# Two attentions ahead of a feed-forward layer, on one core: groups of 1920 tokens in four lanes of 480, turned by VectorE, in place of units of 960 turned by TensorE

## The chip, the cores and the metric

The kernel runs on one core of one Trainium2 chip. A core has five engines with a queue each: TensorE (PE, with its weight load PEld), VectorE (DVE), ScalarE (ACT), GpSimd (POOL) and SyncE (SP, which here only issues DMAs). Each executes its queue in the order in which the program wrote it. The metric is the device time of one execution in microseconds. The kernel before has a median of 1677.85 us over three runs (1677.34 to 1679.97).

## The reference

Four batches of 12480 tokens with 128 channels; 32 inducing vectors; a feed-forward layer with 2048 inner channels.

```python
def mab(q, kv):                       # softmax attention, keys = values
    s = scale * (q @ kv.transpose(0, 2, 1))
    s = s - s.max(-1, keepdims=True)
    a = np.exp(s)
    a /= a.sum(-1, keepdims=True) + 1e-09
    return a @ kv
h = mab(I, x)                         # first attention: 32 queries over 12480 tokens
attn = mab(x, h)                      # second: every token over the 32 rows of h
y = np.maximum(attn @ w_in, 0.0)
out = y * y @ w_out
```

The weights come as 64-bit floats. The first attention of a batch has to be complete (its softmax runs over all tokens) before the second can begin for any token of that batch.

## The kernel before

**Folding.** The second attention's output is `a @ h`, a weighted sum of 32 rows. So the kernel never forms it: once a batch's h is known, `first_end` computes hw = h x w_in (32 x 2048, L635 to L644), and the feed-forward layer's first product is a x hw with the 32 attention weights of each token as inputs. For accuracy the weights stand as high and low parts, stacked four times 32 on 128 partitions (the tile st), and hw likewise. In the second product w_out and the activations are split into high and low parts too, and three of the four products are summed.

**Tiling.** Each batch is 13 units of 960 tokens (UNIT = NT x TS = 8 x 120). A unit has four lanes of 240 tokens for the attentions, and two blocks of 480 tokens for the feed-forward layer, 104 blocks in all.

**First attention of a unit** (class First). SP loads x as 120 partitions x 8 rows of 512 B (xn, L426). The channels have to be on the partitions for the scores: the first batch's x is turned by PE (L466) and copied by ACT; later batches load 32 x 32 blocks (xb, L444) which VectorE transposes (xt, L448, 128 x 960). Four matmuls give the scores of the four lanes on 4 x 32 partitions (L481). Each lane has a running maximum of its own: VectorE's max (L494) and neg (L500), ACT's exp with its sum (L507) and the factor `fade` by which earlier sums shrink (L510). PE turns e (ep, L515), ACT copies it (et, L274), 16 matmuls add e x x per lane (`mix`, L539), and VectorE adds it up (hacc L551, zs L561).

**End of a batch** (`first_end`). The four lanes are merged: their maxima gathered (L587 to L595), a factor per lane (wq, L599), the total (L607 to L614) and the joining matmul (L622). Then hw.

**Second attention of a unit** (class Second). Scores from hT (L677), evicted by ACT (ss, L274), turned by PE (s2t, L696), then VectorE's max (mx, L703), sub (d, L707), ACT's exp (L710), VectorE's total (z, L714), POOL's z + 1e-9 (L718), reciprocal (L721) and norm (L724) on 120 x 256; PE turns them back (ap, L755), ACT or VectorE writes the high part (L274) and VectorE the low part (L765) of sw, 128 x 240 each. SP spreads sw to st by 16 DMAs of 32 x 240 (L771). Only the very first unit goes another way: its high and low parts are made ahead of turning back (sk, L732 and L736), the matmul that turns them also stacks them (L741), and ACT copies the result to st, with no DMA.

**Feed-forward layer of a block** (`ffn_block`). 16 matmuls of 480 columns give h (L899). ACT does relu (L912, 960 wide) and square (L928, 1920 wide); VectorE makes hi (L933) and lo (L938), 1920 wide, four of each per block; 48 matmuls add up op (L977); VectorE turns it (ob, L993) and SP stores it with four DMAs (L999).

**What sets the order.** Nothing is issued where it is written. Each piece is a task of one `Plan`, with an engine or a choice of two, an assumed length, a due time, its needs and the buffers that it takes. `Plan.run` simulates the engines and, per engine, takes of the tasks that could start at about the same time the one due first. The resulting order is the order of the queues. The feed-forward blocks have due times from a base (T_MAIN) and a period; within a block HI_DUE, LO_DUE, SQ_DUE and others offset them.

Of the kernel before, what the change touches and what calls it, by code (L numbers as in the profile page):

```python
# [165 lines left out]
def induced_attention_then_squared_relu_ffn(  # L166
# [13 lines left out]
    NP = NF // 2  # L180
    NU = N // UNIT
    Q = P // M
    scale = 1.0 / math.sqrt(C)
    NQ = NF // 4
    GB, HB, LB = 3, 2, 2
    PERIOD, START, T_MAIN, NARROW, STEP = 30500.0, 2600.0, 44000.0, -9000.0, 3000.0
    W_DUE = [14e3, 20e3, 28e3, 34e3, 50e3, 52e3, 56e3, 60e3]

    XT, OT, ST = ("ACT|DVE", "ACT|DVE"), ("ACT|DVE", "ACT|DVE"), "ACT|DVE"
    XT_EARLY = "ACT"  # L190

    ORDER = "x0 x1 x2 i0 x3 x4 x5 i1 x6 x7 x8 i2 x9 x10 i3 x11 x12 o0 o1 o2 o3".split()
    SPARE = (6, 7, 8)
    FIRST_PAIRS, LAST_PAIRS = 2, 1
    OB, SS, SS_NS = "DVE", "ACT|DVE", (255, 317)

    FUSED = set()
    POOL_HI = set()
    POOL_LO = set()
    FUSED_DUE = 3000.0  # L200
    STICK = 0.0
    JOIN_IN, REST_OUT, JOIN_OUT = "DVE", "DVE", "DVE"
    HALVES = True
    PATIENCE = (0.0, 0.0, 40.0)

    PAIR, PAIR_DUE = False, 3000.0
    MB = 2
    G1_DUE, SQ_DUE, HI_DUE, LO_DUE, OP_DUE = -2000.0, 6000.0, 5000.0, 6000.0, 10500.0
    WIDE_LATER, NEXT_FIRST, STEP_0 = 7000.0, 2000.0, 600.0
    OT_DUE, OTP_DUE, OSB_DUE, XT_DUE, FILL = 4000.0, 4000.0, 10000.0, 1000.0, 0.0  # L210
    LATE_RELU, LATE_HI = 250.0, 50.0
    LATE_G1, LATE_OT = 250.0, 400.0


    const = ctx.enter_context(tc.tile_pool(name="const", bufs=1))
# [28 lines left out]
    identr = const.tile([P, P], F32R, name="identr")  # L244
    nc.vector.tensor_copy(identr, ident)
# [20 lines left out]

    add = plan.add
    ENG = {
        "ACT": nc.scalar.copy, "DVE": nc.vector.tensor_copy,
        "POOL": lambda dst, src: nc.gpsimd.tensor_scalar(dst, src, 1.0, 0.0, ALU.mult, ALU.add),  # L270
    }

    def copy(task, dst, src):
        ENG[task.by](dst, src)  # L274

# [68 lines left out]
    def open_early():  # L344
        pools["hi"] = ctx.enter_context(tc.tile_pool(name="hi", bufs=HB))
        pools["lo"] = ctx.enter_context(tc.tile_pool(name="lo", bufs=LB))
        pools["early_scope"] = ExitStack()
        pools["early"] = pools["early_scope"].enter_context(tc.tile_pool(name="early", bufs=6, side="right"))
# [12 lines left out]
    def load_weights(due):  # L361
# [3 lines left out]
        for k in range(n):  # L365
            sl = slice(k * WCH, (k + 1) * WCH)

            def load(t, sl=sl):
                nc.sync.dma_start(t, w_in[:, sl].bitcast(I32).rearrange("p (n two) -> p n two", two=2))

            def use(v, needs, due, kw, sl=sl):
                def join():
                    on(t).tensor_add(w_in_sb[:, sl], v["a"].bitcast(F32), v["b"])

                t = add(JOIN_IN, length(JOIN_IN), join, due, needs, port=True, **kw)
                return t

            ins.append(weights(f"i{k}", load, use, due[k]))
        for k in range(n):
# [6 lines left out]
            def use(v, needs, due, kw, k=k):  # L386
# [14 lines left out]
                tr = add(REST_OUT, length(REST_OUT), rest, due, [t], port=True, **kw)  # L401
                tj = add(JOIN_OUT, length(JOIN_OUT), join, due, [tr], port=True, **kw)
# [6 lines left out]

    class First:
        def __init__(self, b, u, due, early=False, begun=None):

            self.b, self.u, self.early, self.n, self.begun = b, u, early, f"{b}_{u}", begun
            self.s = s = state.setdefault(b, {"xt": {}, "chain": None, "bxt": {}})
            self.home = "early" if early and u not in SPARE else "xn"
            self.bx = Buffer(self.home)
            self.bt = s["bxt"][u] = Buffer("xt")
            lead = 2500 if early else 8000  # L420

            def load():
                self.xn = (pools["early"] if self.home == "early" else xn_pool).tile(
                    [TS, NT, C], F32, tag="xn", name=f"xn_{self.n}"
                )
                nc.sync.dma_start(self.xn, x_v[b, u])  # L426

            loaded = add("SP", 2050, load, ORDER.index(f"x{u}") * 10.0 - 1000.0 if b == 0 else due - lead - 20000, takes=[self.bx], late=0)
            self.turned = []
            if not early:  # L430
                self.turned.append(self.turn_blocks(due - lead))
                return
# [20 lines left out]

        def turn(self, k, due, loaded):
            bank_ = Buffer("o" if self.early else "m")
            v = {}

            def turn():
                if k == 0:
                    self.xt = self.s["xt"][self.u] = xt_pool.tile([C, UNIT], F32, tag="xt", name=f"xt_{self.n}")  # L460
                if self.early:
                    v["tp"] = ps_o.tile([P, 512], F32, tag="o", name=f"xtp_{self.n}_{k}")
                else:
                    v["tp"] = bank(f"xtp_{self.n}_{k}")
                for t in range(4):
                    nc.tensor.transpose(  # L466
                        v["tp"][:, t * TS:(t + 1) * TS], self.xn[:, 4 * k + t, :], ident[:TS, :TS]
                    )

            def turned():  # L470
                copy(e, self.xt[:, k * BLK:(k + 1) * BLK], v["tp"][:, :BLK])

            t = state["turn"] = add("PE", 421, turn, due, [loaded, state.get("turn"), self.begun] + self.turned, mode="t",
                    takes=[bank_] + ([self.bt] if k == 0 else []), reads=[self.bx] + ([self.bt] if k else []))
            e = add(XT_EARLY if self.early else XT[k], (440, 567), turned, due + (600 if self.early else XT_DUE), [t], reads=[bank_, self.bt])
            return e

        def score(self, where):

            for q in range(Q):  # L480
                nc.tensor.matmul(  # L481
                    where[q * M:(q + 1) * M, :], indT,
                    self.xt[:, q * 2 * TS:(q + 1) * 2 * TS], start=True, stop=True,
                )

        def weigh(self, scored, where, bank_, due, pair=None):

            s, u, n = self.s, self.u, self.n
            v = {}
            prev = s.get("first")  # L490

            def top():
                v["mx"] = tiny.tile([P, 1], F32, tag="mx", name=f"mx_{n}")
                nc.vector.tensor_reduce(v["mx"], where(), axis=AX.X, op=ALU.max)  # L494

            def shift():

                self.neg = tiny.tile([P, 1], F32, tag="neg", name=f"neg_{n}", bufs=4)
                if u:
                    nc.vector.scalar_tensor_tensor(self.neg, v["mx"], -scale, prev.neg, ALU.mult, ALU.min)  # L500
                else:
# [582 lines left out]
```

## Time and profile before

| | |
|---|---|
| median of three runs | 1677.85 us (1677.34 to 1679.97) |
| the profiled execution | 1679.11 us, span in the trace 1677.3 us |
| mean granted TensorE clock | 0.994 |
| moved by DMA | 101.21 MB, mean 60 GB/s |
| feed-forward on VectorE | hi 476.1 us, lo 893.8 us of 1608.4 busy |

The costliest lines of PE and ACT (line, engine, operation, tiles, count, then busy us and mean ns of one, then idle time just before):

```profile
L912 ACT ACTIVATE g<-h 128x960 f32<-128x960 f32 x832 | 786.2, 992 | 30.3 <-PE h L899 18.6
L899 PE MATMUL h<-st,hw 128*128 128x480 f32 x1664 | 515.1, 388 | 7.0 <-ACT g L912 6.2
L977 PE MATMUL op<-lo,wo_hi 128*128 128x480 f32 x1664 | 476.4, 383 | 2.8 <-DVE lo L938 2.8
```

A matmul's duration overlaps its neighbours', so the durations of a PE line do not add up to time. Idle time of an engine that is not the bottleneck costs nothing. In groups of lines the number before the comma is the sum of durations, and on VectorE the durations overlap a little too.

### The profile page before, as it was taken

What the parts mean: (1) busy time and instruction counts of PE and PEld (TensorE: products, weight loads), DVE (VectorE), ACT (ScalarE), POOL (GpSimd) and SP (SyncE); (2) the same over time, 40 slices, a digit from 0 to 9 for tenths busy, and PEclk for the clock granted to TensorE, in tenths of its full rate; (3) what the DMA queues carried; (4) which work ended last, traced back from release to release, by engine and by line L of the source; (5) the groups of instructions that cost most, each with busy time, mean ns of one, the idle gap of its engine ahead of it and who ended that gap; (6) DMA issues with size and microseconds to landing.
All of it is one profiled execution on the core that took longest, in us unless ns stands there. A gap on an engine that the chain in (4) does not pass through costs nothing.

```text
span 1677.3 us, 24531 instructions
## 1 busy us (share of the span) xinstructions
PE 1631.7 (97%) x8799; PEld 1340.5 (80%) x8799; DVE 1608.4 (96%) x1619; ACT 1564.8 (93%) x1657; POOL 77.6 (5%) x57
## 2 busy tenths in 40 slices
PE   6699999999999999999999999999999999999998
PEld 4378888888878888888877888888887888888886
DVE  4899999999999999999999999999999999999998
ACT  5599999999989999999998999999998999999996
POOL 0000000000000000000000000000000000000000
PEclk9899999999999999999999999999999999999999
DMA  9733333323243334334324334334111111212121
GB/s 201 136 61 64 72 57 70 68 56 72 52 65 63 70 61 68 62 67 73 61 48 70 63 68 72 61 69 66 34 33 35 30 32 35 38 31 42 26 44 21
DMA packets 451380, 101.21 MB, mean 60 GB/s; under 512 B 372636, under 2 KB 450748, under 8 KB 451260
## 3 DMA queue, kind: packets, MB, share of 16 engines
q1 hardware_dynamic: 451260, 99.66, 33.2%
q8 instruction: 70, 1.15, 0.3%
q14 instruction: 50, 0.41, 0.1%
HBM read 48.94 MB, written 25.56 MB: 44 GB/s over the span
## 4 chain that ended last, share of the span: by engine, by line
PE 76%; DVE 12%; issue 5%; ACT 3%; DMA 2%; SPq 2%; DVEq 0%; ACTq 0%
PE op L977 52%; PE h L899 18%; DVE lo L938 5%; DVE hi L933 4%; PE na L677 1%; ACT g L912 1%; SPq L426 1%; PE nb L539 1%; ACT g L928 1%; PE na L481 1%; DMA hi_i<-in_moe_w_in_dram 1%; DMA xn<-in_x_dram 1%; SPq L771 1%; DMA xb<-in_x_dram 1%; PE s2t L696 1%
## 5 line engine op out<-in xcount | busy, mean ns | idle before, releaser
L938 DVE TENSOR_TENSOR lo<-g,hi 128x1920 fp32r<-128x1920 f32 (+1 forms) x419 | 893.8, 2134 | 15.9 <-DVE hi L933 0.5
L912 ACT ACTIVATE g<-h 128x960 f32<-128x960 f32 x832 | 786.2, 992 | 30.3 <-PE h L899 18.6
L928 ACT ACTIVATE g<-g 128x1920 f32<-128x1920 f32 (+1 forms) x419 | 763.4, 1823 | 3.4
L899 PE MATMUL h<-st,hw 128*128 128x480 f32 x1664 | 515.1, 388 | 7.0 <-ACT g L912 6.2
L933 DVE CAST hi<-g 128x1920 fp32r<-128x1920 f32 (+1 forms) x419 | 476.1, 1137 | 6.7 <-ACT g L928 6.1
L977 PE MATMUL op<-lo,wo_hi 128*128 128x480 f32 x1664 | 476.4, 383 | 2.8 <-DVE lo L938 2.8
L977 PE MATMUL op<-hi,wo_lo 128*128 128x480 f32 x1664 | 454.1, 382 | 0.0
L977 PE MATMUL op<-hi,wo_hi 128*128 128x480 f32 x1664 | 451.4, 385 | 2.1 <-DVE hi L933 1.9
L899 PEld LDWEIGHTS h<-st,hw 128*128 128x128 f32 x1664 | 307.1, 188 | 77.6 <-issue 15.2
L977 PEld LDWEIGHTS op<-lo,wo_hi 128*128 128x128 f32 x1664 | 309.1, 188 | 59.5 <-DVE lo L938 10.9
L977 PEld LDWEIGHTS op<-hi,wo_lo 128*128 128x128 f32 x1664 | 311.3, 188 | 49.8
L977 PEld LDWEIGHTS op<-hi,wo_hi 128*128 128x128 f32 x1664 | 307.7, 188 | 53.5 <-DVE hi L933 6.0
L718 POOL TENSOR_SCALAR z<-z 120x8 f32<-120x8 f32 x51 | 76.9, 1508 | 1536.5 <-DVE z L714 1536.5
L993 DVE STREAM_TRANSPOSE ob<-op 128x480 f32<-128x480 f32 (+1 forms) x105 | 70.2, 669 | 3.8 <-PE op L977 3.7
L448 DVE STREAM_TRANSPOSE xt<-xb 128x960 f32<-128x960 f32 x39 | 45.6, 1170 | 1.5 <-DMA xb<-in_x_dram 1.5
L274 ACT COPY ss<-na 128x240 f32<-128x240 f32 x52 | 19.4, 374 | 25.0 <-PE na L481 13.9
L539 PE MATMUL nb<-xn,et 120*32 120x128 f32 x752 | 33.1, 280 | 0.0
L677 PE MATMUL na<-xt,hT 128*32 128x240 f32 x416 | 32.7, 387 | 0.4 <-DVE hT L274 0.4
L539 PEld LDWEIGHTS nb<-xn,et 120*32 120x32 f32 x752 | 25.0, 110 | 7.2 <-issue 0.2
L274 ACT COPY xt<-xtp 128x480 f32<-128x480 f32 x26 | 14.5, 557 | 14.9 <-PE xtp L466 14.9
L515 PE MATMUL ep<-ident,e 128*120 128x128 f32 x104 | 20.7, 281 | 6.3 <-ACT e L507 6.3
L274 ACT COPY et<-ep 120x256 f32<-120x256 f32 x52 | 19.6, 378 | 6.8 <-PE ep L515 6.6
(107 smaller groups left out, 542.8 us busy)
## 6 DMA issues: line engine op xcount, KB each, us to landing
xn<-in_x_dram SPq DMA_DIRECT2D x52, 480.0 KB, 5.3
out_dram<-ob SPq DMA_DIRECT2D x412, 60.0 KB, 2.0
st<-sw SPq DMA_DIRECT2D x816, 30.0 KB, 1.8
xb<-in_x_dram SPq DMA_DIRECT2D x156, 120.0 KB, 3.6
hi_i<-in_moe_w_in_dram SPq DMA_DIRECT2D x2, 512.0 KB, 10.6
lo_i<-in_moe_w_in_dram SPq DMA_DIRECT2D x2, 512.0 KB, 11.0
hi_o<-in_moe_w_out_dram SPq DMA_DIRECT2D x2, 512.0 KB, 10.1
lo_o<-in_moe_w_out_dram SPq DMA_DIRECT2D x2, 512.0 KB, 7.7
```

The source lines that it names most:

```text
L274: ENG[task.by](dst, src)
L448: nc.vector.transpose(self.xt, v["xb"].rearrange("p r c -> p (r c)"))
L539: nc.tensor.matmul(where[q * M:(q + 1) * M, :], self.et[:, k, q * M:(q + 1) * M], self.xn[:, 2 * q + k, :], start=(k == 0), stop=(k == 1),)
L677: nc.tensor.matmul(where[q * M:(q + 1) * M, :], self.s["hT"][:, :M], self.s["xt"][self.u][:, q * 2 * TS:(q + 1) * 2 * TS], start=True, sto ...
L718: E.tensor_scalar(v["z"], v["z"], 1e-9, 0.0, ALU.add, ALU.add)
L899: nc.tensor.matmul(c["hp"][:, l, :BLK], s["hw"][:, f * P:(f + 1) * P], s["st", u][:, 2 * k:2 * k + 2].rearrange("p q k t -> p (q k t)"), s ...
L912: nc.scalar.activation(g, h, AF.Relu)
L928: nc.scalar.activation(v["g"][:, h], v["g"][:, h], AF.Square)
L933: ENG[by](v["hi"][:, h], v["g"][:, h])
L938: engine.tensor_sub(v["lo"][:, h], v["g"][:, h], v["hi"][:, h])
L977: nc.tensor.matmul(w["op"][:, :BLK], wo[:, 4 * j + l, :], v[name][:, l, :], start=(j == x == 0 and l == 0), stop=(j == NQ - 1 and x == 5 a ...
L993: nc.vector.transpose(w["ob"][:, rows].rearrange("p r c -> p (r c)"), w["op"][:, rows.start * S:rows.stop * S])
```

## The change

- A batch is now 6 groups of 1920 tokens and one of 960. A group has up to four lanes of 480 tokens, and a lane is a block of the feed-forward layer. x comes as 15 whole rows per partition (7680 contiguous bytes, L399).
- First attention (L495 to L564): one step for 1920 tokens. The running maximum is one for all lanes: after VectorE's max (top, L502) the lanes' maxima are spread by `lanes` (L506), gathered by a small matmul with `same` (L509), reduced (most, L513) and shifted (L520). e is turned by VectorE (L540) instead of by PE and ACT. 15 matmuls mix (L548).
- End of a batch (L587 to L624): since all lanes share a maximum, the merging of lanes falls away.
- Second attention (L657 to L705): scores of 128 x 480, turned by VectorE straight from PSUM (L664), max, sub, exp, total, norm on 128 x 480, turned back by VectorE (L692), high and low parts 480 wide, and four DMAs of 32 x 480 per lane. Each lane has a tile st of its own. The last group of a batch, 960 tokens, takes four lanes of 256 of which two overlap.
- The very first block has a short chain of its own (`mini`, four lanes of 128). It is spread by 16 DMAs which ACT's queue issues.
- The first batch's x is still turned by PE (15 turns per group, L437); its evictions may go to ACT or VectorE.
- The planner's numbers are set anew: HI_DUE from 5000 to 3000, LO_DUE from 6000 to 6500, OP_DUE from 10500 to 10300, PATIENCE, the loads' order and due times; xt has 14 half buffers, st six, `early` three, xn two, and a, sw one.

The diff, cut to its core:

```diff
-TS = 120
-NT = 8
-UNIT = TS * NT
-BLK = UNIT // 2
 S = 32
-NR = BLK // S
+NR = 15
+LANE = S * NR
...
-    G1_DUE, SQ_DUE, HI_DUE, LO_DUE, OP_DUE = -2000.0, 6000.0, 5000.0, 6000.0, 10500.0
+    G1_DUE, SQ_DUE, HI_DUE, LO_DUE, OP_DUE = -1500.0, 6000.0, 3000.0, 6500.0, 10300.0
+    PATIENCE = (20000.0, 60000.0, 40.0)
...
+                nc.sync.dma_start(
+                    self.xn[:R], x[b, self.at:self.at + self.L * LANE, :].rearrange("(p r) c -> p r c", r=NR)
+                )
...
+            def lanes():
+                v["lanes"] = tiny.tile([P, Q], F32, tag="lanes", name=f"lanes_{n}")
+                nc.vector.tensor_scalar_mul(v["lanes"][:R], lane_q[:R], v["mx"][:R])
+            def gather():
+                nc.tensor.matmul(v["sp"][:, LANE:LANE + L], same[:R, :], v["lanes"][:R, :L], start=True, stop=True)
+            def most():
+                v["top"] = tiny.tile([P, 1], F32, tag="top", name=f"top_{n}")
+                nc.vector.tensor_reduce(v["top"], v["sp"][:, LANE:LANE + L], axis=AX.X, op=ALU.max)
...
+            def turn_e():
+                self.et = att.tile([P, NR, S], F32, tag="et", name=f"et_{n}")
+                nc.vector.transpose(
+                    self.et[:R].rearrange("p r m -> p (r m)"), v["e"][:R].rearrange("p r t -> p (r t)")
+                )
...
+            def turn():
+                v["d"] = att.tile([P, NR, M], F32, tag="d", name=f"d_{n}")[:RW, :NB, :]
+                nc.vector.transpose(v["d"].rearrange("p r m -> p (r m)"), v["na"][:RW, :W])
...
+            def back():
+                v["a"] = att.tile([P, LANE], F32, tag="a", name=f"a_{n}", bufs=1)[:RW, :W]
+                nc.vector.transpose(v["a"], v["d"].rearrange("p r m -> p (r m)"))
...
+            def spread(k):
+                st = self.st[k] = st_pool.tile([P, LANE], F32R, tag="st", name=f"st_{b}_{g}_{k}")
+                for a in range(4):
+                    for i, c0, c1, d0 in to[k]:
+                        queue(
+                            st[a * M:(a + 1) * M, d0:d0 + c1 - c0].bitcast(F32),
+                            v["sw"][i * M:(i + 1) * M, a % 2, c0:c1].bitcast(F32),
+                        )
+            urgent = tag == "m"
+            queue = nc.scalar.dma_start if urgent else nc.sync.dma_start
```

What it does to the order. VectorE's queue in the middle of a batch, before (hi and lo are the feed-forward splits, ob the output's turn; the first three numbers are unit, block and quarter of the block's 16 inner tiles):

```order
L933 CAST hi_1_0_3_1403<-g_1_0_3_1358 128x1920
L938 TENSOR_TENSOR lo_1_0_3_1420<-g_1_0_3_1358,hi_1_0_3_1403 128x1920
L933 CAST hi_1_1_0_1438<-g_1_1_0_1375 128x1920
L938 TENSOR_TENSOR lo_1_1_0_1448<-g_1_1_0_1375,hi_1_1_0_1438 128x1920
L933 CAST hi_1_1_1_1467<-g_1_1_1_1412 128x1920
L993 STREAM_TRANSPOSE ob_1_0_1481<-op_1_0_1321 128x480
L938 TENSOR_TENSOR lo_1_1_1_1487<-g_1_1_1_1412,hi_1_1_1_1467 128x1920
```

The same queue after, also in the first batch (group in place of unit; lanes, top: first attention of the next batch; mx, d: second attention of this one):

```order
L785 CAST hi_2_2_3_2374<-g_2_2_3_2328 128x1920
L506 TENSOR_SCALAR lanes_3_2384<-lane_q,mx_3_2354 128x4
L668 TENSOR_REDUCE mx_0_4_2386<-d_4_2292 128x15
L790 TENSOR_TENSOR lo_2_2_3_2392<-g_2_2_3_2328,hi_2_2_3_2374 128x1920
L785 CAST hi_2_3_0_2406<-g_2_3_0_2362 128x1920
L513 TENSOR_REDUCE top_3_2415<-sp_3_2311 128x1
L671 TENSOR_TENSOR d_4_2292<-d_4_2292,mx_0_4_2386 128x480
L790 TENSOR_TENSOR lo_2_3_0_2421<-g_2_3_0_2362,hi_2_3_0_2406 128x1920
```

In the first piece a hi is twice followed at once by its own lo; in the second short attention steps stand between the two.

ACT's queue ahead of the first relu of the feed-forward layer, before (hw and wo_hi: folding and weight splits; st: the first unit's attention weights, written by ACT):

```order
L507 ACTIVATE e_1_0_889,z_1_0_888<-na_1_0_871,neg_1_0_885 128x240
L274 COPY et_0_901<-ep_0_896 120x256
L274 CAST st_0_922<-ap_0_0_911 128x4x120
L274 CAST st_0_922<-ap_0_1_916 128x4x120
L391 CAST wo_hi<-lo_o_732 128x512
L274 COPY ss_1_952<-na_1_929 128x240
L912 ACTIVATE g_0_0_0_957<-h_0_0_0_927 128x960
```

and after:

```order
L619 CAST hw_711<-wp_3_749 128x512
L361 CAST wo_hi<-lo_o_595 128x512
L705 DMA st_0_0_782<-sw_0m 32x128 x3
L705 DMA st_0_0_782<-sw_0m 32x96
L705 DMA st_0_0_782<-sw_0m 32x128 x3
L705 DMA st_0_0_782<-sw_0m 32x96
L705 DMA st_0_0_782<-sw_0m 32x128 x3
L705 DMA st_0_0_782<-sw_0m 32x96
L705 DMA st_0_0_782<-sw_0m 32x128 x3
L705 DMA st_0_0_782<-sw_0m 32x96
L767 ACTIVATE g_0_0_0_809<-h_0_0_0_800 128x960
```

Two copies by ACT have become 16 DMA issues on ACT's queue, ahead of the first relu.

SP's queue where the first batch goes over into the second, before (st: attention weights of the second batch's first unit; xb: blocks of x for the third batch, x4 and x16 are counts of DMAs):

```order
L999 DMA out_dram<-ob_11_1_4685 32x15x32 x4
L444 DMA xb_2_4767<-in_x_dram 32x30x32 x4
L771 DMA st_0_4819<-sw_0_4795 32x240 x16
L999 DMA out_dram<-ob_12_0_4881 32x15x32 x4
L426 DMA xn_3_4935<-in_x_dram 120x8x128
```

and after:

```order
L844 DMA out_dram<-ob_5_3_4272 480x1x32 x4
L469 DMA xb_1_0_4340<-in_x_dram 32x15x32 x8
L705 DMA st_0_0_4385<-sw_0_4361 32x480 x4
L705 DMA st_0_1_4393<-sw_0_4361 32x480 x4
L705 DMA st_0_2_4404<-sw_0_4361 32x480 x4
L705 DMA st_0_3_4415<-sw_0_4361 32x480 x4
L844 DMA out_dram<-ob_6_0_4494 480x1x32 x4
```

The 16 DMAs ahead of the next batch's first h have become four for each of its four blocks; eight loads of xb stand ahead of them where four stood.

More of the change, by code (lines that the diff above doesn't have):

```diff
@@ L478, in score @@
[L478 to L490, printed above, removed]
+            t = state["turn"] = add("DVE", 1090, turn, due, [t, state.get("turn"), self.begun],
+                                    takes=[self.bt[h]], reads=[bb])
@@ new lines, in weigh @@
+            t = add("DVE", wide_ns(LANE), top, due + step, [t, back("shifted")], reads=[bank_])
+            t = add("DVE", 100, lanes, due + step, [t])
+            t = add("PE", 70, gather, due + step, [t], reads=[bank_])
+            t = add("DVE", 100, most, due + step, [t], reads=[bank_])
+            t = self.shifted = add("DVE", 70, shift, due + step, [t])
+            cl = add("POOL", 100, clear, due, [back("totalled")]) if R < P else None
+            t = self.powered = add("ACT", 820, power, due + 2 * step, [t, cl, back("powered")], takes=[be], reads=[bank_])
@@ L661, in first_end @@
             bw = Buffer("m" if b else "h")
[L662 to L664 removed]
+            d = due + 2 * step + k * step
+            t = add("PE", 870, lambda k=k: wide(k), d, [s["joined"], w_ins[k]], takes=[bw])
+            t = add("ACT", 520, lambda k=k: part(k), d, [t], reads=[bw])
@@ L795, in weigh @@
-            t = add("DVE", 340, top, d + max(step, PAIR_DUE if pair else 0), [t], reads=[bt])
-            td = add("DVE", 340, sub, d + max(step, PAIR_DUE if pair else 0), [t], reads=[bt])
-            tp = add("ACT", 307, power, d + 2 * step, [td])
-            t = add("DVE", 330, total, d + 2.5 * step, [tp])
-            ez = add("DVE" if first else "POOL", 150, safe, d + 2.5 * step, [t])
-            t = add("DVE", 120, invert, d + 2.5 * step, [ez])
-            tp = add("DVE", 340, norm, d + 3 * step, [t], port=True)
@@ L816, in weigh @@
-            t = add("PE", 219, back, d + 4 * step, [tp], takes=[ba], mode="t")
-            th = add(ST, (255, 317), high, d + 5 * step, [t], takes=[bw], reads=[ba])
-            tl = add("DVE", 317, low, d + 5 * step, [th], reads=[ba, bw])
-            t = None
-            for q in range(Q):
-                t = add("SP", 2200, lambda q=q: spread(q), d + 6 * step, [tl, t], late=0,
-                        takes=[] if q else [self.bst], reads=[bw] + ([self.bst] if q else []))
-            self.ready = [t] * 2
@@ new lines, in __init__ @@
+            t = add("DVE", ns, turn, d + step, [t], takes=[bd], reads=[bank_])
+            t = add("DVE", ns, top, d + 1.5 * step, [t], reads=[bd])
+            t = add("DVE", ns, sub, d + 2 * step, [t], reads=[bd])
+            t = add("ACT", wide_ns(W, "ACT"), power, d + 3 * step, [t], reads=[bd])
+            t = add("DVE", ns, total, d + 4 * step, [t], reads=[bd])
+            ez = t = add("DVE" if urgent else "POOL", 150, safe, d + 4 * step, [t])
+            t = add("DVE", 100, invert, d + 4 * step, [t])
```

679 lines of the change are left out of this document (274 added, 405 removed).

## The prediction

> **What bounds the kernel now.** I read first the page's totals and slices, then the windows by stage, then VectorE's timeline.
>
> ```profile
> PE 1631.7 (97%) x8799; PEld 1340.5 (80%) x8799; DVE 1608.4 (96%) x1619; ACT 1564.8 (93%) x1657; POOL 77.6 (5%) x57
> DVE  4899999999999999999999999999999999999998
> ```
>
> Three engines are above 93%, so totals do not name the bound; the slices only say that the start is the one loose place. The windows (window, length, busy and count of PE, PEld, DVE, ACT, POOL, granted clock, DMA share, GB/s) split it:
>
> ```profile
> 0.00:11.00 11.00, 4.29 (x22) 2.79 (x23) 1.33 (x8) 2.96 (x4) 0.70 (x6) 1.00 0.86 158
> 11.00:47.00 36.00, 27.50 (x338) 19.42 (x341) 21.77 (x65) 23.33 (x68) 0.00 (x0) 1.00 1.12 225
> 47.00:74.70 27.70, 16.10 (x131) 8.71 (x123) 24.67 (x61) 12.30 (x31) 0.00 (x0) 0.83 0.74 132
> 74.70:102.00 27.30, 24.23 (x122) 17.62 (x123) 22.05 (x27) 23.96 (x30) 1.08 (x1) 0.92 0.25 43
> 102.00:455.00 353.00, 351.75 (x1928) 290.53 (x1927) 349.58 (x351) 338.97 (x349) 16.96 (x11) 1.00 0.36 66
> 455.00:525.00 70.00, 67.22 (x347) 53.40 (x346) 66.23 (x70) 61.69 (x69) 3.42 (x3) 0.98 0.38 64
> 832.00:894.00 62.00, 59.73 (x317) 46.80 (x315) 58.13 (x64) 53.60 (x58) 0.24 (x1) 1.00 0.34 59
> 1204.00:1330.00 126.00, 124.53 (x622) 101.48 (x621) 121.22 (x115) 118.52 (x118) 5.50 (x4) 1.00 0.17 32
> 1330.00:1671.00 341.00, 339.91 (x1617) 283.86 (x1615) 331.49 (x276) 327.47 (x306) 14.86 (x10) 1.00 0.18 34
> ```
>
> In the main phase (102 to 455) PE and VectorE both have 99%. Which of them waits, the timeline tells (start, duration, engine, line):
>
> ```profile
> 249.54 2.16 DVE L938 TENSOR_TENSOR lo<-g,hi 128x1920 fp32r<-128x1920 f32 x1
> 251.62 1.15 DVE L933 CAST hi<-g 128x1920 fp32r<-128x1920 f32 x1
> 252.88 2.16 DVE L938 TENSOR_TENSOR lo<-g,hi 128x1920 fp32r<-128x1920 f32 x1
> 254.95 1.15 DVE L933 CAST hi<-g 128x1920 fp32r<-128x1920 f32 x1
> 256.02 0.67 DVE L993 STREAM_TRANSPOSE ob<-op 128x480 f32<-128x480 f32 x1
> 256.62 2.12 DVE L938 TENSOR_TENSOR lo<-g,hi 128x1920 fp32r<-128x1920 f32 x1
> ```
>
> Each instruction starts about 0.08 us before the one ahead ends: lo 252.88 to 254.95 is 2.07, duration 2.16; the transpose 0.60 for 0.67. So an instruction costs its duration less 0.08; I call that its slot. The one exception is a hi followed at once by its own lo: 251.62 to 252.88 is 1.26, against 1.07 for the next hi, which has a transpose behind it. In the main phase VectorE's instructions add up by slots to the elapsed time, 61.2 us for every four blocks, so **VectorE's queue is the bound** there, and PE is fed just in time. Outside it VectorE is short of work at the start (11 - 1.33 = 9.7, then 14.2, 3.0 and 5.3: 32.2 us), at three batch turns (3.8, 3.9 and 4.8 us) and in the last batch (9.5 of 341).
>
> **The change, by VectorE's slots.** Rows that price it (busy, mean ns | idle before):
>
> ```profile
> L938 DVE TENSOR_TENSOR lo<-g,hi 128x1920 fp32r<-128x1920 f32 x413 | 887.0, 2148 | 15.8 <-DVE hi L933 0.5 <-PE op L977 0.5
> L938 DVE TENSOR_TENSOR lo<-g,hi 128x960 fp32r<-128x960 f32 x6 | 6.8, 1152 | 0.0
> L993 DVE STREAM_TRANSPOSE ob<-op 128x480 f32<-128x480 f32 x103 | 69.5, 674 | 3.0 <-PE op L977 2.9
> L703 DVE TENSOR_REDUCE mx<-s2t 120x8 f32<-120x256 f32 x52 | 21.7, 417 | 3.1 <-PE s2t L696 2.8
> L714 DVE TENSOR_REDUCE z<-d 120x8 f32<-120x256 f32 x52 | 21.1, 406 | 0.5 <-ACT d L710 0.5
> L765 DVE TENSOR_TENSOR sw<-ap,sw 128x240 fp32r<-128x240 f32 x51 | 20.3, 399 | 0.7 <-ACT sw L274 0.7
> L494 DVE TENSOR_REDUCE mx<-na 128x1 f32<-128x240 f32 x39 | 15.4, 394 | 0.3 <-ACT ss L274 0.3
> L551 DVE SCALAR_TENSOR_TENSOR hacc<-hacc,fade,nb 128x128 f32<-128x128 f32 x43 | 14.5, 337 | 0.3
> L561 DVE SCALAR_TENSOR_TENSOR zs<-zs,fade,z 128x1 f32<-128x1 f32 x44 | 9.3, 211 | 3.2 <-ACT fade L510 3.1
> L721 DVE RECIPROCAL z<-z 120x8 f32<-120x8 f32 x52 | 9.2, 176 | 0.5 <-POOL z L718 0.4
> L500 DVE SCALAR_TENSOR_TENSOR neg<-mx,neg 128x1 f32<-128x1 f32 x48 | 7.2, 151 | 0.0
> L274 DVE CAST sw<-ap 128x240 fp32r<-128x240 f32 x14 | 5.6, 401 | 0.1
> L587 DVE TENSOR_SCALAR lanes<-lane_q,neg 128x4 f32<-128x4 f32 x4 | 0.9, 219 | 0.0
> L595 DVE TENSOR_REDUCE negt<-lp 128x1 f32<-128x4 f32 x4 | 0.6, 158 | 0.5 <-PE lp L591 0.4
> ```
>
> *Removed.* First attention, 52 units: maximum 52 x 0.315 = 16.4, hacc 13.1, zs 6.6, neg 52 x 0.07 = 3.6, together 39.7. Second attention: max, sub and norm 52 x 3 x 0.337 = 52.6, total 52 x 0.326 = 17.0, reciprocal 5.0, low 51 x 0.319 = 16.3, high 14 x 0.32 = 4.5, the first unit's sk about 1.0: 96.4. The merging of lanes at a batch's end about 1.3. Sum **137.4**.
>
> *Added.* Between the two lo rows an element costs (2148 - 1152) / 960 = 1.04 ns, so a 480-wide maximum is 394 + 250 - 80 = 0.564 us, sub, norm, total and low 0.56 to 0.57; a 480 transpose is the output's, 0.594. First, 28 groups: maximum 0.564, lanes 0.139, most 0.078, neg 0.07, turned e 0.594, hacc 0.257, zs 0.131: 1.83 each, 51.3. (A last group of a batch has half the lanes but the same width, so its maximum and turn save nothing.) Second, 24 full groups: two transposes, max, sub, total, norm, low, reciprocal: 4.11 each, 98.7; four half groups of 256 width 2.51 each, 10.0; the small first chain 1.7; high on VectorE 1.8. Eleven and eight evictions of the first batch's turned x, 5.8. Sum **169.3**, so +31.9. None of the 480-wide transposes from SBUF stands in the trace; bounds are the 0.33 us slot of a 256-wide row and a second 0.594: 80 of them at -0.26 to +0.6 would be -21 to +48. The output's row has their very width, so I take it, and allow +-8.
>
> *Won by order.* By the program's order 165 of the 413 wide hi stood directly ahead of their own lo; now 61 do, since short attention steps lie between. 104 x 0.19 = **-19.8**. So VectorE's own work rises by 12.1, and nearly all of that lies ahead of the fifth block; the main phase stays as it is.
>
> The Trainium skill, "VectorE: DVE Perf Modes", section "Rules for kernel authors", says the contrary of this step: a drain follows every VectorE instruction however instructions are chained, so that only their number matters. The 1.26 against 1.07 above disagrees; by the page the sum would be 19.8 higher.
>
> *PE and ACT* lose work: the turns of e and scores through PE with their evictions. That is off VectorE's queue and I cost it at nothing; cover is VectorE itself.
>
> *Start.* Loads of x come in 512 B rows before and in 7680 B pieces after. Two windows, x alone and w_out:
>
> ```profile
> 38.00:42.00 4.00, 2.93 (x38) 1.81 (x38) 1.93 (x6) 2.58 (x8) 0.00 (x0) 1.00 1.16 186
> 44.00:50.00 6.00, 3.72 (x51) 2.45 (x51) 4.39 (x13) 4.61 (x15) 0.00 (x0) 1.00 1.08 311
> ```
>
> The first batch is 6.4 MB: 34 us at 186 GB/s, 21 at the other rate. Of the 14.2 us idle in 11 to 47 I let 8 go. Against that the first block was handed from PSUM by ACT alone; now it crosses by 16 DMAs on ACT's queue. Their price is SyncE's (issue min/median/max ns, landing us):
>
> ```profile
> L771 SPq DMA_DIRECT2D st<-sw x816: 507/588/1849, 90.1 to 1629.6; - x164
> DMA to landing us min/median/max: 1.7/1.8/3.8
> 467.57 11.76 SPq L771 DMA_DIRECT2D st<-sw  x16
> ACT ss L274 <- PE na L481: 4.3, 1, 4.3
> ```
>
> 16 x 0.588 = 9.4, landing 1.8, relu and exp queued on ACT behind the issues 2.4, less 3.4 of loose work for VectorE, so the third window's idle goes from 3.0 to about 11, the fourth from 5.3 to 4, the first stays: 9.7 + 6.2 + 11 + 4 = 30.9, **-1**.
>
> *Turns.* At 467.57 the second batch's first spread issues 16 DMAs in 11.8 us (row three), and ACT waits 4.3 us at once (row four). Now the four DMAs of lane 0 suffice, 2.4 us, so the next h may start some 9 us sooner; the eight loads of xb stand ahead of them on SyncE, 4.7 us, and by the order the attention's last VectorE step has 3 to 4 us less VectorE work between itself and the next batch's first hi (13.5 us for 17.5 at the first turn). The three windows lack 12.5 us of busy VectorE, plus the lost overlaps of 0.08, say 14; I leave 1 us per turn: **-11**. In the last batch, 9.5 idle in 341 is 2.8% against 1.0% in the main phase, an excess of 6; half of it goes, **-3**.
>
> Sum: +12.1 - 1 - 11 - 3 = -2.9 on the profiled execution's 1679.1 (span 1677.3 and 1.8 around it): 1676.2. That execution is 1.25 above the median of the runs, 1677.85, so **1675.0**.
>
> **Rivals.**
> *Loads no quicker.* The 8 us at the start stay: 1683. It needs x to come at 186 GB/s whatever the row. The 311 of the next window, where rows are longer, speaks against it; that these are other tensors, for it. The Trainium skill, "DMA: Bandwidth & Descriptors", section "Specifications", puts the least size for line rate at 512 B, by which the old rows lost nothing. The rate of 186 disagrees.
> *Slower: the handoff on ACT's queue.* All of the first h waits for 16 issues, and ACT issues nothing else meanwhile. At 1.2 us each it is 19.2 instead of 9.4: 1685; at the row's largest, 1.849, 20 more: 1695. It decides from (6.2 + 9.4) / 16 = 0.98 us each, where the time passes 1681.2. For it: no DMA issued by ACT is in the trace, and w_out's splits are still on ACT. Against: the median.
> *Order wins nothing.* If hi's 0.19 is paid by whatever comes next, 19.8 are lost: 1695. The row of the 1.07 speaks against it. (It is the first page's rule.)
> *PE is the bound after all.* Then its lost turns shorten the main phase:
>
> ```profile
> L515 PE MATMUL ep<-ident,e 128*120 128x128 f32 x104 | 20.7, 281 | 6.3 <-ACT e L507 6.3
> L696 PE MATMUL s2t<-ident,ss 128*120 128x128 f32 x104 | 20.1, 275 | 0.0
> L755 PE MATMUL ap<-ident,d 120*128 120x120 f32 x102 | 18.9, 266 | 0.0
> ```
>
> 59.7 us of overlapping durations, some 40 net, less what more VectorE work takes back: about -23, 1652. The fit by slots speaks against it.
> *A quick handoff.* At 0.35 us an issue and less idle elsewhere in the start, -11: 1664.
>
> **How the numbers follow.** Chances: forecast 0.57 (own range 1667 to 1683, mostly from the transposes' +-8), loads 0.12, handoff 0.11, order 0.08, PE 0.07, quick handoff 0.05. For 0.8 I leave out PE's case and the upper ends beyond 1692: 1659 to 1692. What a measurement here can tell from no change is 0.2%, that is 1674.5 to 1681.2. Of the forecast's 0.57 I put 0.29 below, 0.20 within, 0.08 above; loads 0.04 within and 0.08 above; handoff 0.02 and 0.09; order 0.01 and 0.07; PE and quick handoff 0.12 below, less 0.01 within. Faster 0.40, same 0.28, slower 0.32.
>
> **What would show it.** Slots of 0.59 for the new transposes, and of 0.56 to 0.57 for the other 480-wide steps; a hi with a step between it and its lo at 1.07; x at near 300 GB/s from 11 us on; 16 ACT-issued DMAs in about 9.4 us ahead of the first h; the first output's turn near 102 as before; turns at which VectorE lacks about 1 us. I am wrong if the main phase, with VectorE full all the same, moves away from 61 us per four blocks, or if the first h stands far from the 74.7 us at which the third window ends.

## The result, and the profile after

| | before | after |
|---|---|---|
| median | 1678.38 us (1677.34 to 1679.97, 4 runs) | 1688.18 us (1685.36 to 1689.74, 4 runs) |
| profiled execution | 1679.11, span 1677.3 | 1689.74, span 1687.9 |
| mean granted clock | 0.994 | 0.982 |

The ratio is 1.0056 (95% interval 1.0038 to 1.0073): the change is slower by about 10 us, where 1675.0 was forecast. The time lies inside the stated range, on the wrong side of no change. One execution of a later run (two buffers sw) took 2633.84 us at a granted clock of 0.557, for 1680.63 to 1684.8 of its other nine; its ratio leaves that one out.

The page's totals after, then the same windows as before:

```profile
PE 1629.7 (97%) x8146; PEld 1299.7 (77%) x8146; DVE 1623.4 (96%) x1524; ACT 1533.8 (91%) x1443; POOL 72.0 (4%) x38
DVE  7699999999999999999999899999999999999998
```

```profile
11.00:47.00 36.00, 30.39 (x336) 18.59 (x328) 31.81 (x92) 18.66 (x53) 0.10 (x1) 0.96 0.71 217
47.00:74.70 27.70, 12.83 (x74) 4.84 (x74) 21.81 (x49) 6.31 (x13) 0.00 (x0) 0.62 0.24 79
74.70:102.00 27.30, 16.10 (x44) 11.59 (x45) 15.35 (x19) 15.64 (x18) 1.44 (x2) 0.63 0.31 58
102.00:455.00 353.00, 352.68 (x1808) 286.86 (x1807) 351.30 (x316) 338.44 (x313) 13.93 (x6) 1.00 0.33 68
1330.00:1671.00 341.00, 337.58 (x1524) 279.28 (x1517) 331.64 (x255) 329.35 (x290) 15.80 (x5) 0.99 0.17 33
```

VectorE is full again in the main phase, and fuller in the second window (31.8 us busy for 21.8). Over the third and fourth together it lacks more (17.8 us for 8.3). PE's granted clock is 0.62 and 0.63 there, with PE busy 12.8 and 16.1 us; before it was 0.83 and 0.92, with 16.1 and 24.2. What that clock costs was not taken apart.

Windows cut the stages at the old boundaries, so a second reading is wanted: how much work VectorE's queue holds up to a given output, and how long it took. I give every VectorE instruction its slot (start to start, by form; 0.19 us more where it reads what the one just ahead wrote), add them up in queue order to each block's output turn, and set that beside the turn's end in the trace. What is left is idle time of VectorE (us). The split turns on the slots taken: with the median start to start of each form in its own trace, VectorE's work rises by 2.5 in place of the 7.6 below and its idle time by 8.6 in place of 3.5, so single entries hold to some 5 us.

| up to | before: work | idle | after: work | idle |
|---|---|---|---|---|
| first block's output | 69.6 | 33.0 | 83.5 | 32.0 |
| 24th, just ahead of the first turn | 423.8 | 31.8 | 434.4 | 31.8 |
| 32nd, behind the first turn | 549.6 | 36.1 | 558.8 | 36.9 |
| 56th, behind the second | 922.4 | 39.7 | 928.5 | 41.4 |
| 84th, behind the third | 1340.9 | 43.2 | 1356.1 | 42.4 |
| last | 1625.7 | 45.6 | 1633.3 | 49.1 |

Work rose by 7.6 and idle by 3.5: 11.1, which is the difference of the last output's turn (1682.4 against 1671.3). Up to the first turn the sums are as forecast: more work and the start's idle about the same. But the turns still cost 10.6 (11.4 before) where 1 each had been expected, and the last batch 6.7 for 2.4. With the other slots the turns cost 11.5 (9.5 before) and the last batch 7.2 for 2.3, so by either count the forecast gain is missing.

What waits there, by VectorE's own waits in the trace of after (us in total, times, longest):

```profile
DVE z L678 <- ACT d L674: 11.3, 1, 11.3
DVE xt L241 <- ACT xt L241: 6.8, 5, 4.7
DVE hi L785 <- ACT g L780: 5.4, 7, 1.5
DVE sw L241 <- DMA st<-sw: 4.5, 2, 3.8
DVE xt L472 <- DMA st<-sw: 4.5, 2, 3.2
DVE xt L472 <- DMA xb<-in_x_dram: 2.7, 1, 2.7
```

The first row is the handoff at the start. The last three are new or larger (before, only 1.5 us for xb): VectorE, the bound engine, waits for DMAs that SyncE issues. Behind the first turn, VectorE and then SyncE (SPq: DMA issues) in the trace of after:

```profile
531.19 1.15 DVE L785 CAST hi<-g 128x1920 fp32r<-128x1920 f32 x1
535.50 1.18 DVE L472 STREAM_TRANSPOSE xt<-xb 128x960 f32<-128x960 f32 x1 [3.16 <-DMA st<-sw]
```

```profile
518.33 9.53 SPq L705 DMA_DIRECT2D st<-sw  x12
527.95 5.28 SPq L469 DMA_DIRECT2D xb<-in_x_dram  x8
533.33 1.20 SPq L705 DMA_DIRECT2D st<-sw  x2
```

The eight loads of xb stand in SyncE's queue behind twelve spreads, which take 9.5 us to issue. The last of them is issued at 533.2 and lands some 2 us later, when VectorE's turn begins. The trace names a spread as what came last; the timeline shows that it is the load behind the spreads. Behind the second turn (932.9 us, 2.7 for xb) the eight loads wait for the one buffer xb, which VectorE's turn at 924.4 empties, and the next turn comes before they have landed. In the last batch it is the other way round: the last lane's spread stands behind a store that waits for its output, and sw has one buffer (two in the kernel before), so VectorE can't write the next sw:

```profile
1545.46 2.47 SPq L705 DMA_DIRECT2D st<-sw  x4
1557.29 2.61 SPq L844 DMA_DIRECT2D out_dram<-ob  x4
1560.00 2.47 SPq L705 DMA_DIRECT2D st<-sw  x4
```

```profile
1559.22 1.15 DVE L785 CAST hi<-g 128x1920 fp32r<-128x1920 f32 x1
1564.22 0.29 DVE L241 CAST sw<-a 128x256 fp32r<-128x256 f32 x1 [3.85 <-DMA st<-sw]
```

The planner made that order, assuming that a lane's four spreads take 0.8 us (2.5 here), eight xb loads 2.05 (5.3) and four stores 0.4 (2.6). Before, these numbers stood at 2.2 for four spreads, 2.05 for four loads and 2.0 for the stores, and the trace of before had 2.35 (four at its median of 0.588), 2.25 and 2.15. The prediction did not weigh that part of the diff.

### The profile page after: what moved, and what is told of

Same layout as the page of the kernel before. It is cut to its first block, busy times and chain, and to the rows that moved or that the text cites. A ratio compares the mean times of both kernels' runs of the same rounds, so it can differ in the third digit from the quotient of the medians.

```text
span 1687.9 us, 22599 instructions
## 1 busy us (share of the span) xinstructions
PE 1629.7 (97%) x8146; PEld 1299.7 (77%) x8146; DVE 1623.4 (96%) x1524; ACT 1533.8 (91%) x1443; POOL 72.0 (4%) x38
## 3 DMA queue, kind: packets, MB, share of 16 engines
q1 hardware_dynamic: 388976, 99.89, 28.3%
## 4 chain that ended last, share of the span: by engine, by line
PE 81%; DVE 10%; ACT 3%; issue 3%; DMA 2%; SPq 1%; ACTq 0%; DVEq 0%; POOL 0%
PE op L818 57%; PE h L760 19%; DVE lo L790 5%; DVE hi L785 2%; PE nb L548 1%; ACT g L767 1%; PE sp L495 1%; PE na L657 1%; ACT g L780 1%; DMA st<-sw 1%; PE wp L615 1%; PE xtp L437 0%; SPq L705 0%; DVE hw L624 0%; DVE xt L241 0%
## 5 line engine op out<-in xcount | busy, mean ns | idle before, releaser
L767 ACT ACTIVATE g<-h 128x960 f32<-128x960 f32 x832 | 781.4, 973 | 87.6 <-PE h L760 41.4
L818 PE MATMUL op<-lo,wo_hi 128*128 128x480 f32 x1664 | 465.6, 389 | 10.9 <-DVE lo L790 10.5
L682 POOL TENSOR_SCALAR z<-z 128x15 f32<-128x15 f32 (+1 forms) x28 | 70.9, 2531 | 1374.4 <-DVE z L678 1374.4
L548 PE MATMUL nb<-xn,et 128*32 128x128 f32 (+1 forms) x840 | 31.7, 285 | 5.0 <-DVE et L540 5.0
L495 PE MATMUL sp<-xt,indT 128*32 128x480 f32 x208 | 32.0, 610 | 4.1 <-DVE xt L241 2.6
L548 PEld LDWEIGHTS nb<-xn,et 128*32 128x32 f32 (+1 forms) x840 | 23.7, 113 | 14.5 <-DVE et L540 7.5
L241 ACT COPY xt<-xtp 128x256 f32<-128x256 f32 (+1 forms) x33 | 11.1, 366 | 21.1 <-PE xtp L437 17.8
L678 DVE TENSOR_REDUCE z<-d 128x15 f32<-128x480 f32 (+1 forms) x28 | 17.1, 612 | 11.3 <-ACT d L674 11.3
L657 PE MATMUL na<-xt,hT 128*32 128x480 f32 (+1 forms) x224 | 26.8, 557 | 0.0
L530 ACT ACTIVATE e<-sp,neg 128x480 f32<-128x480 f32 (+1 forms) x28 | 18.5, 660 | 4.6 <-DVE neg L520 3.5
## 6 DMA issues: line engine op xcount, KB each, us to landing
hi_i<-in_moe_w_in_dram SPq DMA_DIRECT2D x2, 512.0 KB, 10.6
```

What stands on the lines that cost most here:

```text
L495: nc.tensor.matmul(v["sp"][q * M:(q + 1) * M, :LANE], indT, s["xt"][self.g, q // 2][:, q % 2].rearrange("c r t -> c (r t)"), start=True, s ...
L548: nc.tensor.matmul(v["nb"][c * M:(c + 1) * M, :], self.et[:R, r, :], self.xn[:R, r, :], start=r < Q, stop=r >= NR - Q,)
L657: nc.tensor.matmul(v["na"][i * M:(i + 1) * M, :W], s["hT"][:, :M], s["xt"][gg, h][:, l].rearrange("c r t -> c (r t)")[:, c:c + W], start=T ...
L682: E.tensor_scalar(v["z"], v["z"], 1e-9, 0.0, ALU.add, ALU.add)
L767: nc.scalar.activation(v["g"][:, 2 * i:2 * i + 2, :], c["hp"][:, :, :LANE], AF.Relu)
L818: nc.tensor.matmul(w["op"][:, :LANE], wo[:, 4 * j + l, :], v[name][:, l, :], start=(j == x_ == 0 and l == 0), stop=(j == NQ - 1 and x_ == ...
```

## The experiments

Each run had runs of the kernel before on the same chip beside it (medians 1679.0 to 1679.6). The change was timed beside 1678.38, and the runs here on three chips, so a difference of two medians below is uncertain by about 1 us.

### One more buffer xb

```diff
-    GB, HB, LB, OB, MB, STB, XTB, XNB, XBB = 3, 2, 2, 2, 2, 6, 14, 2, 1
+    GB, HB, LB, OB, MB, STB, XTB, XNB, XBB = 3, 2, 2, 2, 2, 6, 14, 2, 2
```

> The changed kernel with two buffers xb instead of one. Theory A (SyncE's issues came too late): VectorE's waits for xb at 531 us (3.2) and 929 us (2.8) go, 6 us less than the changed kernel's 1688.2, so 1682. Rival B (the time went into VectorE's own larger attention work ahead of the first output, 13.9 us more): no change, 1688 within 2.

Measured 1692.33 us (1691.36 to 1693.39), ratio to before 1.0075 (1.006 to 1.0091): 4 slower, against both theories. The first turn did get cheaper (idle 1.3 us from the 24th to the 32nd output, for 5.1). But the planner used the buffer to queue more loads at the start, and SyncE in this run's timeline does 19 of them ahead of the first full spreads (14 in the change, where these spreads begin 3.6 us sooner, at 94.96):

```profile
79.59 18.88 SPq L469 DMA_DIRECT2D xb<-in_x_dram  x19
98.56 8.50 SPq L705 DMA_DIRECT2D st<-sw  x12
```

The idle ahead of the first output is 37.9 us for 32.0, and a wait of 3.6 us for xb stands there now. So this buffer alone did not help; the wait moved. That the loads ahead of the spreads cost all of the 5.9 us is not shown.

### One more buffer sw

```diff
-                v["sw"] = att.tile([P, 2, LANE], F32R, tag="sw", name=f"sw_{n}", bufs=1)
+                v["sw"] = att.tile([P, 2, LANE], F32R, tag="sw", name=f"sw_{n}", bufs=2)
```

(and the planner's count likewise)

> The changed kernel with two buffers sw instead of one. Theory A: the waits for sw in the last batch (3.9 at 1559, 0.9 and 0.8 at 1445 and 1503) go, 4 to 5.6 us less, so 1683 to 1684. Rival B: 1688 within 2.

Measured 1683.32 us, ratio 1.0022 (1.0012 to 1.0031): 4.9 less than the change, as the theory has it. That the waits for sw are what went is argued from the time alone; no trace of this run shows it.

### SyncE's measured lengths

```diff
-            t = state["blocks"] = add("SP", 2050, load, due - 20000, ...
+            t = state["blocks"] = add("SP", 5300, load, due - 20000, ...
-  add("ACT" if urgent else "SP", 250 if urgent else 800, lambda k=k: spread(k), ...
+  add("ACT" if urgent else "SP", 250 if urgent else 2450, lambda k=k: spread(k), ...
-            add("SP", 400, lambda rows=rows: store(rows), end + 6000, [t])
+            add("SP", 2600, lambda rows=rows: store(rows), end + 6000, [t])
```

> The changed kernel, planned with the lengths of SyncE's tasks that its trace shows (a lane's four spreads 2.45 us instead of 0.8, eight xb loads 5.3 instead of 2.05, four stores 2.6 instead of 0.4); nothing else. Theory A: loads and spreads stand in an order in which they come in time, and most of the 7 to 11 us of new waits go without a buffer more: 1677 to 1682. Rival B: 1688 within 2. Rival C (one buffer each is too few whatever the order): no more than 2 us less.

Measured 1671.47 us (1669.89 to 1671.86), ratio 0.9949 (0.9935 to 0.9964): 16.7 less than the change and 8 less than before. Not an instruction was added: the page counts 1524 on VectorE in both. The edit changes only three assumed lengths, but the planner orders every queue by them, so VectorE's and ACT's orders differ from the change's too. The loads now stand ahead of the spreads, and behind the first turn SyncE's timeline of this run reads:

```profile
505.85 5.27 SPq L469 DMA_DIRECT2D xb<-in_x_dram  x8
511.22 2.61 SPq L844 DMA_DIRECT2D out_dram<-ob  x4
515.68 11.60 SPq L705 DMA_DIRECT2D st<-sw  x16
```

and VectorE's waits:

```profile
DVE z L678 <- ACT d L674: 11.1, 1, 11.1
DVE xt L241 <- ACT xt L241: 6.8, 6, 4.4
DVE sw L241 <- DMA st<-sw: 1.9, 3, 0.9
```

No wait for xb is left. By the count of slots the three turns cost -0.9 us together (28.3 idle ahead of the first, 27.4 behind the third), the last batch 2.5, the start 28.2. Idle time can't be less than nothing: that is the error of the slots. Against the change that is 11.5 less at the turns, 4.2 in the last batch and 3.8 at the start. Rival B is refuted: VectorE's work here is even 1 us larger than in the change (1634.3). That larger work is real, but it is not what kept the time up. Rival C is refuted as well: with one buffer each, 16.7 us went.

### Both, and parts of the lengths

Two buffers xb besides (the line of the first experiment):

> Both: two buffers xb and the measured lengths. Theory A: 1676 to 1681, little beyond the lengths alone, since they heal the same waits. Rival C: as with two xb alone, 1682. Rival B: 1688 within 2.

1670.40 us (1669.1 to 1671.26), ratio 0.9942 (0.9926 to 0.9959): 1 us less, within the theory. With the right order, the buffer that cost 4 us before costs nothing.

The xb loads' length alone:

> The changed kernel with the measured length of the xb loads alone (5.3 for 2.05), spreads and stores as in the changed kernel (0.8 and 0.4). If the xb loads' assumed length is what spoiled the order: 1676 to 1680. If it was the spreads' and stores' lengths, which the diff cuts from 2.2 and 2.0 to 0.8 and 0.4: 1685 to 1690.

1686.10 us (1685.13 to 1687.92), ratio 1.0041 (1.0026 to 1.0056): the second case; these alone are not enough. The eight loads stand behind sixteen spreads here:

```profile
520.24 11.07 SPq L705 DMA_DIRECT2D st<-sw  x16
531.41 5.28 SPq L469 DMA_DIRECT2D xb<-in_x_dram  x8
```

The spreads' and stores' lengths of before alone (800 to 2200, 400 to 2000):

> The changed kernel with the two SyncE lengths that the diff cuts set back to those of before (a lane's spreads 2.2 for 0.8, a block's stores 2.0 for 0.4). If these two numbers are what took back the gain at the turns and in the last batch: 1670 to 1674. If it takes all three measured lengths: 1678 to 1687.

1678.61 us (1676.94 to 1680.99), ratio 0.9995 (0.9986 to 1.0005): in the second case, at its lower end. It takes back 9.6 of the change's 9.8 us; the other 7 came only with all three measured lengths, which also raise these two a little. The same eight loads stand behind four spreads:

```profile
516.22 3.17 SPq L705 DMA_DIRECT2D st<-sw  x4
519.74 5.86 SPq L469 DMA_DIRECT2D xb<-in_x_dram  x8
```

Its first turn costs -0.2 of idle, but between the 48th and the 56th output 5.5 us still go, with one wait of 3.1 for xb. So at the first turn the place of the loads and the cost go together: behind sixteen or twelve spreads VectorE's idle time from the 24th to the 32nd output is 7.5 and 5.0 us, behind four or none nothing (with the slots of each trace's own medians).

### Is VectorE's queue the bound?

The low part of sw written twice by VectorE, in the kernel before:

```diff
                 nc.vector.tensor_sub(v["sw"][:, 1], v["ap"][:, :2 * TS], v["sw"][:, 0])
+                nc.vector.tensor_sub(v["sw"][:, 1], v["ap"][:, :2 * TS], v["sw"][:, 0])
```

> The kernel before with VectorE's low part of sw written twice (51 more instructions of 0.319 us). If VectorE's queue is the bound throughout: +16, so 1695. If PE is: within 3 of before, 1679.

1699.27 us (1697.75 to 1699.86), ratio 1.0117 (1.01 to 1.0134): +20.3, or 0.40 per instruction added; VectorE's added work is paid in full. That is more than the slot of 0.319: in this run's trace the second low starts 0.435 us after the first, though it only overwrites what the first wrote.

PE's turns of the scores done twice, in the kernel before:

```diff
-                for k in range(2):
+                for k in (0, 1, 0, 1):
```

> The kernel before with PE's turns of the scores (s2t) done twice (104 more matmuls of 0.14 to 0.28 us each). If VectorE's queue is the bound: 0 to +4, so 1679 to 1683. If PE is: +14 or more, 1693 and up.

1686.01 us (1685.46 to 1687.22), ratio 1.004 (1.0026 to 1.0054): +7, between the cases. VectorE's work is the same (1625.7) and its idle 52.6 for 45.6; of the 7 more, 1.8 arise up to the 24th output and the rest behind the 32nd. So PE has room for most of this in the first batch, but not all through; about half of the least price is paid.

### Does a step between hi and lo save time?

In the version with measured lengths, hi is moved down to directly ahead of its own lo:

```diff
+    for lo in [t for t in line if hasattr(t, "hi")]:
+        i, k = line.index(lo.hi), line.index(lo)
+        if any(t.by == "DVE" for t in line[i + 1:k]) and not any(lo.hi in t.needs for t in line[i + 1:k]):
+            line.insert(k - 1, line.pop(i))
```

> The version with measured SyncE lengths, with hi moved down to directly before its own lo wherever no product stands between: 351 adjacent pairs for 63. By the trace's slots (1.25 against 1.07): 288 x 0.18 = +52, so 1723. Rival (each VectorE instruction pays its drain anyway, and only their number counts): within 4 of 1671.5.

1732.91 us (1731.42 to 1734.45), ratio 1.0318 (1.0301 to 1.0335). That is 61.4 more than its base for 288 more pairs, 0.21 each, with the same number of VectorE instructions. VectorE's timeline of this run:

```profile
306.59 1.16 DVE L785 CAST hi<-g 128x1920 fp32r<-128x1920 f32 x1
307.85 2.16 DVE L790 TENSOR_TENSOR lo<-g,hi 128x1920 fp32r<-128x1920 f32 x1
309.93 0.65 DVE L678 TENSOR_REDUCE z<-d 128x15 f32<-128x480 f32 x1
```

hi to its own lo is 1.26; lo to a step that does not need it 2.08, for a duration of 2.16. The step that reads what was just written pays; by the run before, one that overwrites it pays too (0.435). Waits are no rival: VectorE's idle time by slots is within about 1 us of the base's.

### Did contiguous loads help the start?

The first batch's x in rows of 512 B again, in the version with measured lengths (this permutes that batch's tokens, as the expectation says):

```diff
-  x[b, ...].rearrange("(p r) c -> p r c", r=NR)
+  x[b, ...].rearrange("(r p) c -> p r c" if early else "(p r) c -> p r c", r=NR)
```

> The version with measured SyncE lengths, in which the first batch's x is loaded again as rows of 512 B (which permutes that batch's tokens: its second attention and outputs belong to other rows; the work is the same). If contiguous loads gave the start 8 us: 1679. If rows of 512 B come as fast: within 2 of 1671.5.

1671.41 us (1670.99 to 1671.61), ratio 0.9952 (0.9935 to 0.9968): no difference to its base, and the start's idle is 28.3 for 28.2. The same window of this run and of the change (last column GB/s; 207 in the kernel before; mostly loads of x, some of w_in):

```profile
3.00:9.00 6.00, 1.89 (x8) 1.57 (x8) 0.40 (x2) 0.37 (x1) 0.00 (x0) 1.00 1.15 290
```

```profile
3.00:9.00 6.00, 2.86 (x12) 2.31 (x13) 0.85 (x2) 0.74 (x2) 0.00 (x0) 1.00 0.99 393
```

The contiguous rows do come faster, 393 for 290 GB/s. PE's turns of x wait 9.1 us for them in rows of 512 B and 6.2 in the base, but VectorE, which bounds, gains nothing from it.

### The handoff of the first block

Half of the 16 spreads go to SyncE, in the version with measured lengths:

```diff
-                        queue(
+                        (nc.sync.dma_start if urgent and a % 2 else queue)(
```

> The version with measured SyncE lengths, in which half of the first block's 16 spreads (the four low-part halves' two) are issued by SyncE and half by ACT. Theory (16 issues in a row hold the first h, 10.3 us): the wait of 11 us at 71 us shrinks by 4 to 5, so 1666.5 to 1667.5 for 1671.5. Rival (landing or PE's low granted clock sets it): within 1 of 1671.5.

1665.49 us (1664.5 to 1666.53), ratio 0.9919 (0.9902 to 0.9935): 6.0 less than its base. The issue rows, of the change (16 by ACT) and of this run (8 by each):

```profile
68.77 10.33 ACTq L705 DMA_DIRECT2D st<-sw_0m  x16
```

```profile
65.80 5.09 ACTq L705 DMA_DIRECT2D st<-sw_0m  x8
66.69 5.14 SPq L705 DMA_DIRECT2D st<-sw_0m  x8
73.17 1.94 PE L760 MATMUL h<-st,hw 128*128 128x480 f32 x4 [10.62 <-DMA st<-sw_0m]
```

VectorE's wait for the exp behind the issues goes from 11.1 to 5.8 us, and the first h starts at 73.2 us for 79.7. The rival of the low clock falls: in the window 47 to 74.7 the granted clock is 0.63 here and 0.71 in the base.

Two buffers sw besides:

> The split handoff with two buffers sw as well: the last batch's remaining waits for sw (0.4 + 0.8 + 1.0) go, 1 to 2 us less than 1665.5. If the planner moves other waits in: 1665 to 1668.

1664.48 us (1663.13 to 1664.79), ratio 0.9909 (0.9894 to 0.9924): the fastest version here, 15 us less than before, in the change's tiling. The difference to the run without the buffer, 1 us, is about the spread of the runs, so the theory of 1 to 2 us is not told from its rival.

## Why the prediction was wrong

- **The bound: right in the main.** VectorE's added work is paid in full, PE's partly (7 of the 14 us or more that PE as the bound would have cost). The main phase stayed where it was: 60.2 to 60.5 us per four blocks from the 4th to the 20th output, 61.2 before.
- **Durations of the new steps: right.** The 480-wide transposes, in groups of lines of the change, last 663 to 670 ns, less 0.08 a slot of 0.58 to 0.59 (0.594 was taken, with a range of 8 us either way for nothing better than the output's row):

```profile
L540 DVE STREAM_TRANSPOSE et<-e 128x480 f32<-128x480 f32 x24 | 16.1, 670 | 0.0
L692 DVE STREAM_TRANSPOSE a<-d 128x480 f32<-128x480 f32 x24 | 16.0, 667 | 0.0
L664 DVE STREAM_TRANSPOSE d<-na 128x480 f32<-128x480 f32 x24 | 15.9, 663 | 0.1
L790 DVE TENSOR_TENSOR lo<-g,hi 128x1920 fp32r<-128x1920 f32 x413 | 881.7, 2135 | 6.4 <-PE op L818 0.5
```

- **VectorE's work: +12.1 forecast, +7.6 counted.** The sum had its sign and place right (+10.6 up to the 24th output), its size 4.5 too large, within what the choice of slots moves. One term it took as unchanged shows in the last row above: the wide lo add up to 881.7 us, for 887.0 before.
- **Order of hi and lo: right.** 0.18 to 0.21 per pair. The Trainium skill, "VectorE: DVE Perf Modes", section "Rules for kernel authors", by which only the number of instructions would matter, disagrees: 61 us were measured at an equal number.
- **Start: right in sum, wrong in its parts.** Idle ahead of the first output went from 33.0 to 32.0 (-1 forecast). By the four windows VectorE lacks 8.4, 4.2, 5.9 and 12.0 us, where 9.7, 6.2, 11 and 4 were forecast; that the sum of 30.4 is so near the 30.9 is partly luck. The 8 us were not won by contiguous rows: with rows of 512 B the start is the same. VectorE is fuller in the second window of after, 31.8 us, with loads, work and buffers all moved; which of them did it was not taken apart. The handoff's issues cost about what was forecast (10.33 us for 16, 9.4 in the sum). But of the signs that the prediction named, two failed: the first h starts at 81.6 us in place of 74.7, and the first output's turn ends at 115.6 in place of near 102.
- **Turns: -11 forecast, -0.8 measured. This is the step that failed.** The prediction priced the spreads on SyncE at the turn's own first block, "the four DMAs of lane 0 suffice, 2.4 us", and "the eight loads of xb stand ahead of them". It did not follow the queue to the next group, where the same loads stand behind twelve spreads, nor ask what lengths the planner assumed for these issues. At the turns themselves about half of the gain came. In the prediction's three windows VectorE lacks 1.8, 2.0 and 3.5 us after the change, 7.3 for 12.5:

```profile
455.00:525.00 70.00, 68.63 (x341) 52.00 (x339) 68.24 (x67) 63.15 (x60) 3.52 (x2) 1.00 0.26 55
832.00:894.00 62.00, 61.76 (x311) 48.19 (x310) 59.95 (x61) 56.78 (x57) 0.32 (x1) 1.00 0.24 51
1204.00:1330.00 126.00, 125.57 (x607) 101.38 (x609) 122.46 (x103) 120.87 (x111) 3.42 (x2) 1.00 0.15 27
```

  Just behind the first two it was lost again, to loads of xb that came late: 3.2 and 2.8 us are lacking there after the change (first two rows), 0.4 and 0.8 before (last two):

```profile
525.00:545.00 20.00, 17.23 (x77) 11.79 (x77) 16.84 (x14) 14.98 (x14) 0.00 (x0) 0.91 0.51 91
894.00:940.00 46.00, 43.18 (x220) 34.10 (x219) 43.22 (x38) 41.85 (x36) 2.13 (x1) 0.95 0.31 66
525.00:545.00 20.00, 20.00 (x119) 16.64 (x118) 19.62 (x19) 19.33 (x18) 0.00 (x0) 1.00 0.27 54
894.00:940.00 46.00, 45.41 (x235) 38.06 (x236) 45.16 (x42) 45.22 (x47) 3.17 (x2) 1.00 0.33 58
```

  The forecast's gain was there to be had: with the measured lengths these five windows lack 4.1 us for 13.7 before, 9.6 less, and by the slots the turns cost 12.3 less.
- **Last batch: -3 forecast, +4.3 measured.** The same kind of step failed, a queue of SyncE not followed: a spread behind a store that waits, and one buffer sw. Even with the lengths mended it is 2.5, against 2.4 before, so little was to be won there by the slots: of the 6 us of excess read from the window's busy share about half was the gap between a hi and its own lo directly behind (58 of the 94 hi of that window, 28 of 93 in the main phase; 30 more at 1.26 less 1.15 are 3.3), which the slots count as work.

With the turns and the last batch as measured, the forecast's other terms give +12.1 - 1 - 0.8 + 4.3 = +14.6, and with the counted work +10.1, against the 10.6 by which the spans differ. The two terms that failed, -14 forecast and +3.5 measured, miss by 17.5; the forecast as a whole missed by 13.5, since the work came out smaller.

## What to carry to other kernels

Where a planner sets the order, the lengths it assumes are part of the change: compare each with the trace, on the queues that only issue DMAs too, since an issue of 0.6 us that is believed to take 0.1 to 0.2 put loads behind spreads here, and the bound engine waited for them. When a change cuts the DMAs at one place, follow that queue through a whole period and ask of each transfer what stands ahead of it. A buffer more may or may not mend a wrong order: one more sw took off 4.9 us here, one more xb added 4.

## What was not expected of the hardware

- A DMA issued by ACT costs as much as one by SyncE here: median 602 ns for the first block's 16 (546 to 727), 588 for SyncE's spreads in the same trace (507 to 1864), and both queues issue side by side at that pace (8 in 5.09 and 8 in 5.14 us).
- Rows of 512 B do not by themselves hold loads at the 186 GB/s that the kernel before showed for x: loads of 960 KB over 128 partitions, in the same rows, came at 290. What held those of 480 KB over 120 partitions at 186 was not tried.
